# A fused FFT, squared-ReLU and mixture-of-experts kernel: w_out read back further ahead, stored rows started sooner, writes moved to earlier batches

## The chip, the core and the metric

The kernel runs on one core of one Trainium2 chip. A core has five engines, each with its own instruction stream: TensorE (PE: matrix products; PEld is its weight load), VectorE (DVE), ScalarE (ACT), GpSimd (POOL) and SyncE (SP). SP does no arithmetic here; it issues nearly all the DMAs, in program order. The metric is the device time of one execution in microseconds (us), lower is better.

## What is computed

The reference runs three stages one after the other on 8 batches of 3072 rows by 256 columns:

```python
X = np.fft.rfft(x, axis=1)                       # x: 8 x 3072 x 256
Yr, Yi = Xr @ w_r - Xi @ w_i + b_r, Xr @ w_i + Xi @ w_r + b_i
# soft threshold: sign(Y) * max(|Y| - 0.01, 0)
x = np.fft.irfft(Yr + 1j * Yi, n=3072, axis=1)   # 24576 rows
h = np.maximum(x @ w_in, 0.0)                    # w_in: 256 x 2048
x = (s * (h * h) + b) @ w_out                    # w_out: 2048 x 256
logits = x @ w_gate                              # 8 experts, capacity 768 each
# row i goes to expert argmax(logits[i]) while that has room, in order of i:
# out[i] = gate_w[i] * (max(x[i] @ w1[e], 0) @ w2[e]); rows beyond the capacity stay zero
```

Most rows end as zeros, so the kernel needs the exact middle stage for few rows. For all other rows it computes only a bounded estimate of the logits in low precision, and it clears the output by writing zeros.

## The kernel before

The main loop runs over 8 batches (b = 0 to 7), each of 64 **units**. A time in the program is written here as batch.unit: 6.42 is unit 42 of batch 6. One unit is one call of `s_unit`: four matrix products into a two-bank tile `ph` (line 786), ReLU of it on ACT into `r` (line 791), and the square on DVE into `qb` (line 792). The pool `hp` has two such tiles, and the inverse transform's tile `pi2` comes from the same two. Every eighth unit the logits are added up (`lg`, lines 806 and 809), copied by ACT to `ls`, and turned (`plt`, line 830).

Between the units stands other work, put there by a table of times. `put(at, f, rank)` enters a step `f` for a unit, and at each unit the loop first emits `s_unit`, then flushes stores left over from earlier steps (`later`), then runs the steps entered for that unit in order of rank and time. Each engine runs its own part of that sequence strictly in order. The planner's function `best` chooses, within two or three units, the one with the least booked PE work (`load[n]`) for the inverse transform (`i2_do`) and for the logits.

The steps beside the units are these.

- `groups(b + 2)`: twelve groups per batch of the transforms of a later batch. A group loads a tile `zp` from memory (line 280), makes products `pf`, `pmx`, `pi`, and stores a tile `v` (line 412). Those of batch 7 end near 6.40, after which batches 6 and 7 have only units and the work below.
- `i2_load` (line 422) loads the input `u` of the inverse transform (three buffers), and `i2_do` does it: 64 small PE instructions (line 438), a cast `ah` on ACT (line 441), two transposes on DVE (line 453), and four DMA stores of `ad` (line 458). In batch 6 the first two loads of batch 7 stand together at unit 55 (`INV_LOAD_AT`).
- Zero writes: 96 DMAs of 256 KB clear the output (line 2061), at the units in `ZERO_AT`: none in batches 0 and 1, ten in each of batches 2 to 5, 31 in batch 6 and 25 in batch 7.
- `save_in` (line 1680): four DMAs of 1 MB write the first layer's weights to memory for a rarely used path, at 6.44, 6.48, 6.52 and 6.56.
- At 6.42 (`P2_AT`) `second` frees the transforms' memory. `load_p2` then reads `w_out` back from memory in eight parts `cf` of 256 KB through three buffers. Each part goes through one cast on ACT (line 1223) and one subtraction on DVE (line 1224) into `wo`, as a high and a low half. Loads 0 and 1 are entered at 6.43 and 6.44, part k is used at 6.42 + 1 + 1.4 (k + 2), and `use(k)` issues load k + 2. When all eight are there, `g0` makes a tile of ones and `g` sums the columns of `wo` with 32 products in a row (`pbc`, line 1237); the sum `yb` is needed by the stored rows.
- Stored rows: `s_items` has 36 steps, four of start-up and 32 that do work, spread evenly between `S_FROM` (7 units before batch 7) and `S_TO` (7.62). Step k loads a tile `sq` (line 1462, three buffers shared with `cf`) for step k + 4, splits that of step k + 2 (ACT line 1469, DVE line 1470, `ssh` and `ssl`), and makes 12 products `ya` (line 1483).
- After the last unit a tail follows: routing, the experts' products, and the final scatter.

The scheduler sets a wait on SP between a DMA and the one eight DMAs before it, since it hands out eight semaphores in turn. So SP has at most eight DMAs of its queue under way, and a wait of one DMA holds all that stand behind it.

Of the kernel before, what the change touches and what calls it, by code (L numbers as in the profile page):

```python
# [10 lines left out]
F32 = mybir.dt.float32  # L11
F32R = mybir.dt.float32r
# [3 lines left out]
ALU = mybir.AluOpType  # L16
# [3 lines left out]
C = 256  # L20
# [6 lines left out]
NF = FF // 128  # L27
# [9 lines left out]
XT = NA * N2  # L37
# [84 lines left out]


FFT_CONV_AT = (0, 2, 5, 7, 10, 12, 13, 18, 20, 23, 25)
S_FROM, S_TO = -7, 62
P2_AT = 42
LIST_AT = 56
SAVE_AT = (44, 48, 52, 56)
TAIL_WARM = 3
XP = 3  # L130
INV_LOAD_AT = 55
# [5 lines left out]
LAST_STEPS = (("g_a", 0), ("g_b", 2), ("g_b2", 3), ("g_soft", 3.1), ("g_c", 5))  # L137
FIRST_STEPS = (("g_a", 0.3), ("g_b", 1.3), ("g_b2", 2), ("g_soft", 2.6), ("g_c", 5))
WORK = {"g_a": 0.87, "g_b": 1.72, "g_b2": 0.86, "g_soft": 0.0, "g_c": 0.86}
ZERO_AT = ((), (), *[tuple(range(4, 64, 6))] * 4, tuple(range(2, 64, 2)), tuple(range(8, 58, 2)))  # L140
LOGIT_LAG = 3
FIRST_LAG = 13
FIN_LAG = 2
# [13 lines left out]
class Kern:  # L157
# [1050 lines left out]
    def load_p2(self, p2):  # L1208

        nc = self.nc  # L1210
        self.wo = p2.tile([128, 2, NF, C], F32R, tag="wo", name="wo")
        st = {}

        def load(k):
            st[k] = self.p2c.tile([128, 512], F32, tag="sq", name="cf", bufs=3)
            nc.sync.dma_start(out=st[k], in_=self.wd[k])

        def use(k):
            if k + 2 < 8:
                load(k + 2)  # L1220
            s = slice(2 * k, 2 * k + 2)
            w = st.pop(k).rearrange("p (k c) -> p k c", k=2)
            nc.scalar.copy(out=self.wo[:, 0, s], in_=w)
            nc.vector.tensor_tensor(out=self.wo[:, 1, s], in0=w, in1=self.wo[:, 0, s].bitcast(F32), op=ALU.subtract)
        it = [lambda: load(0), lambda: load(1)] + [lambda k=k: use(k) for k in range(8)]

        def g0():
            t = self.p2c.tile([128, C], F32, tag="ys", name="ones3", bufs=2)
            nc.vector.memset(t, 1.0)
            st["ones"] = self.p2c.tile([128, 4, 128], F32R, tag="ssh", name="ones4", bufs=2)[:, 0]  # L1230
            nc.scalar.copy(out=st["ones"], in_=t[:, :128])

        def g():
            ps = self.psum("pbc")
            for f in range(NF):
                for w in range(2):
                    nc.tensor.matmul(ps[:, :C], st["ones"], self.wo[:, w, f], start=(f + w == 0), stop=(f == NF - 1 and w == 1))
            self.yb = p2.tile([128, C], F32, tag="yb", name="yb")
            nc.vector.tensor_scalar(out=self.yb, in0=ps[:, :C], scalar1=self.wb, scalar2=None, op0=ALU.mult)
        return it + [g0, g]  # L1240

    def full_pick(self, p2):

# [214 lines left out]

    def s_load(self, k):
        m, f = divmod(4 * k, NF)  # L1460
        t = self.p2c.tile([128, 4, 128], F32, tag="sq", name="sq", bufs=3)
        self.nc.sync.dma_start(out=t, in_=self.sd[f:f + 4].rearrange("f p n -> p f n")[:, :, 128 * m:128 * (m + 1)])
        self.sq[k] = t

# [371 lines left out]
    def run(self):  # L1836
        tc, nc, B = self.tc, self.nc, self.B
# [5 lines left out]
        with ExitStack() as es, tc.manual_schedule():  # L1843
# [79 lines left out]

            nzi, nzn = 0, sum(map(len, ZERO_AT))
            nz = B * S * C // (128 * 512)
# [30 lines left out]
            def put(at, f, rank=1):  # L1956
                e = plan.setdefault(int(at), [])
                e.append((rank, at, len(e), f))
# [14 lines left out]
            load = [0.7] * (64 * B + 80)  # L1973
# [26 lines left out]
            def plan_batch(b):  # L2000
                u = 64 * b
# [15 lines left out]
                        put(n, lambda k=k: self.x_ahead(12 + k), 0)  # L2017
                    put(18, lambda: self.x_ahead(15 + XP), 0)
                if b == B - 2:
                    for n in range(64 + S_FROM + 4, 64 + S_TO):  # L2020
                        load[u + n] += 0.7
                if b == B - 2:
                    for k, n in enumerate(SAVE_AT):
                        put(u + n, lambda k=k: self.save_in(k), 6)
                if b == 0:
# [8 lines left out]
                for i in range(8):  # L2034
                    at = u + 8 * i + 7 + LOGIT_LAG if b + i else FIRST_LAG
                    if b > 1:
                        at = best(u + 8 * i + 9, u + 8 * i + 11, 1.0)
                    if at < 64 * B:
                        put(at, lambda i=i: logits(b, i), 3)
                    if at + FIN_LAG < 64 * B:  # L2040
                        put(at + FIN_LAG, lambda i=i: final(b, i), 2)
                        load[at + FIN_LAG] += 0.4
                    if i < 7 or b + 1 < B:
                        n = best(u + 8 * i + (4 if i < 7 else 3), u + 8 * i + (6 if i < 7 else 5), 1.2, True)
                        put(n, lambda i=i: self.i2_do(*divmod(8 * b + i + 1, 8)), 5)
                    if i < 6:
                        put(u + 8 * i, lambda i=i: self.i2_load(b, i + 2), 0)
                if b == 0:
                    for k in range(8):
                        if k >= CONV_EARLY:  # L2050
# [2 lines left out]
                elif b + 2 < B:  # L2053
                    for k in range(8):
                        put(best(u + 6 * k, u + 6 * k + 4, 1.1, True), self.f1_items(b + 2)[k], 4)
                if b + 1 < B:
                    put(u + INV_LOAD_AT, lambda: (self.i2_load(b + 1, 0), self.i2_load(b + 1, 1)), 2)
                for z in range(len(ZERO_AT[b])):
                    def f(n=sum(map(len, ZERO_AT[:b])) + z):
                        for zi in range(math.ceil(nz * n / nzn), math.ceil(nz * (n + 1) / nzn)):  # L2060
# [3 lines left out]
                if b == 1:  # L2064
                    for m, j in enumerate(XB_AT):
                        w = u + 8 * j
# [13 lines left out]
            def second(at):  # L2080
                e2.close()
                p2 = es.enter_context(tc.tile_pool(name="p2", bufs=1, side="right", reuse_waits="tile"))
                self.p2c = e4.enter_context(tc.tile_pool(name="p2c", bufs=1, side="right", reuse_waits="tile"))
                self.yf = [p2.tile([128, C], F32, tag=f"yf{j}", name=f"yf{j}") for j in range(NJ)]
                u = 64 * (B - 1)
                for n, f in enumerate(self.load_p2(p2)):
                    put(at + 1 + 1.4 * n, f)
                put(at + 3, lambda: self.full_pick(p2))
                for n, f in enumerate(self.full_items(p2)):
                    put(u + 34 + 4 * n, f)  # L2090
                for k in range(4):
                    put(u + 12 + 4 * k, lambda k=k: self.exp_items(self.wx[0], self.fe)[k]())
                for j in range(NJ):
                    put(u + 44 + j, lambda j=j: self.full_gate(j))
                    put(u + S_TO, lambda j=j: self.full_rows(j))
                si = self.s_items()
                for n, f in enumerate(si):
                    put(u + S_FROM + n * (S_TO - S_FROM) / len(si), f)
                put(u + LIST_AT, self.first_block)
                return p2  # L2100
            plan_batch(0)
            for b in range(B):
                if b:
                    plan_batch(b)
                for k in range(64):
                    i, u = divmod(k, 8)
                    if (b, k) == (B - 2, P2_AT):
                        p2 = second(64 * b + k)
# [38 lines left out]
```

## Time and profile before

| | us |
|---|---|
| median of 3 runs | 1466.31 (1463.36 to 1467.7) |
| the profiled execution's own time | 1464.19 |
| its span, first to last instruction | 1462.4 |
| PE busy in the span | 1371.0 (94%) |
| DVE busy | 923.9 (63%) |
| ACT busy | 841.1 (58%) |
| batches 3, 4, 5 and 6, each | 134.0, 134.1, 136.0, 135.2 |
| batch 7's units | 117.0 |

The batches' lengths are the times between the ReLUs that begin them. PE is the busy engine, so the profile is read for the stretches in which PE is not busy, for what ended each wait, and for stretches in which the granted TensorE clock is below 1. A window row gives, for a stretch, its length, then the busy time of PE, PEld, DVE, ACT and POOL with the number of instructions, the granted clock, the mean share in which the 16 DMA engines were busy, and GB/s.

### The profile page before, as it was taken

What the parts mean: (1) busy time and instruction counts of PE and PEld (TensorE: products, weight loads), DVE (VectorE), ACT (ScalarE), POOL (GpSimd) and SP (SyncE); (2) the same over time, 40 slices, a digit from 0 to 9 for tenths busy, and PEclk for the clock granted to TensorE, in tenths of its full rate; (3) what the DMA queues carried; (4) which work ended last, traced back from release to release, by engine and by line L of the source; (5) the groups of instructions that cost most, each with busy time, mean ns of one, the idle gap of its engine ahead of it and who ended that gap; (6) DMA issues with size and microseconds to landing.
All of it is one profiled execution on the core that took longest, in us unless ns stands there. A gap on an engine that the chain in (4) does not pass through costs nothing.

```text
span 1462.4 us, 32413 instructions
## 1 busy us (share of the span) xinstructions
PE 1371.0 (94%) x12865; PEld 1133.7 (78%) x12865; DVE 923.9 (63%) x2151; ACT 841.1 (58%) x1202; POOL 99.9 (7%) x116
## 2 busy tenths in 40 slices
PE   8998799999999989999999999999999799999995
PEld 6876577787788767887888788878888588978884
DVE  1877467666555887677667667766777666664600
ACT  1436545556555656666676666666666677753321
POOL 0000000000000012002000100200020002122020
PEclk9997999999999999999999999999999999999998
DMA  8758476646454447548655865665555788840080
GB/s 236 257 173 237 106 181 171 155 131 170 140 170 121 113 110 184 157 126 187 169 153 146 190 170 131 159 175 153 139 151 162 234 221 237 224 118 16 12 313 13
DMA packets 275842, 234.51 MB, mean 160 GB/s; under 512 B 121661, under 2 KB 229951, under 8 KB 275168
## 3 DMA queue, kind: packets, MB, share of 16 engines
q1 hardware_dynamic: 269984, 226.34, 57.2%
q0 software_dynamic: 3824, 2.82, 0.8%
q10 hardware_dynamic: 1872, 3.18, 0.6%
q8 instruction: 103, 1.69, 0.5%
q14 instruction: 59, 0.48, 0.1%
HBM read 114.17 MB, written 118.29 MB: 159 GB/s over the span
## 4 chain that ended last, share of the span: by engine, by line
PE 70%; DVE 13%; ACT 6%; DMA 5%; issue 3%; SPq 2%; POOL 0%; ACTq 0%; DVEq 0%; POOLq 0%
PE ph L786 20%; PE pmx L368 14%; PE pz L246 5%; PE pi L406 4%; PE pf L291 3%; ACT r L791 3%; PE pi L438 3%; PE phx L1003 3%; PE ya L1483 3%; PE lg L806 2%; DVE qb L792 2%; PE ph L1534 2%; PE po L1544 2%; DMA zp<-zd 2%; PE ya L1018 2%
## 5 line engine op out<-in xcount | busy, mean ns | idle before, releaser
L791 ACT ACTIVATE r<-ph 128x768 bf16<-128x768 f32 (+1 forms) x512 | 399.5, 786 | 208.5 <-PE ph L786 177.8
L786 PE MATMUL ph<-ah,win 128*128 128x384 f32 (+1 forms) x2048 | 480.3, 360 | 20.5 <-ACT r L791 18.8
L792 DVE TENSOR_TENSOR qb<-r 128x768 bf16<-128x768 bf16 (+1 forms) x512 | 272.7, 534 | 245.3 <-ACT r L791 241.3
L786 PEld LDWEIGHTS ph<-ah,win 128*128 128x128 f32 x2048 | 340.6, 191 | 103.9 <-ACT r L791 42.1
L368 PE MATMUL pmx<-wm,l 128*128 128x256 f32 x1196 | 297.9, 387 | 9.4 <-DVE l L299 2.8
L368 PEld LDWEIGHTS pmx<-wm,l 128*128 128x128 f32 x1196 | 223.0, 192 | 41.0 <-ACT r L791 4.3
L940 POOL DMA_INDIRECT list<-c,x x64 | 61.3, 958 | 875.2 <-DVE c L936 858.2
L406 PE MATMUL pi<-t,e 128*128 128x256 f32 x384 | 99.3, 381 | 2.6 <-DVE t L363 1.6
L291 PE MATMUL pf<-d,zp 128*128 128x128 f32 x672 | 88.7, 275 | 1.6 <-DMA zp<-zd 1.5
L291 PEld LDWEIGHTS pf<-d,zp 128*128 128x128 f32 x672 | 85.7, 191 | 2.3 <-DMA zp<-zd 2.1
L246 PE MATMUL pz<-x,f 48*64 48x512 f32 x512 | 74.7, 653 | 10.9 <-DVE at L453 6.6
L438 PEld LDWEIGHTS pi<-f1t,u 48*64 48x64 f32 x4096 | 68.4, 136 | 18.6 <-issue 8.9
L408 ACT COPY v<-pi 128x512 f32<-128x512 f32 x96 | 56.3, 587 | 41.0 <-PE pi L406 37.7
L261 ACT COPY z<-pz 128x1024 f32<-128x1024 f32 x52 | 52.8, 1015 | 46.1 <-PE pz L246 45.9
L453 DVE STREAM_TRANSPOSE at<-pi 128x384 f32<-128x384 f32 x128 | 66.9, 561 | 19.1 <-ACT ah L441 18.0
L406 PEld LDWEIGHTS pi<-t,e 128*128 128x128 f32 x384 | 70.2, 189 | 10.8 <-DVE t L363 3.7
L438 PE MATMUL pi<-f1t,u 48*64 48x48 f32 x4096 | 76.3, 224 | 2.1 <-DMA u<-vd 1.5
L441 ACT CAST ah<-pi 128x768 fp32r<-128x768 f32 x64 | 51.3, 801 | 39.2 <-PE pi L438 39.2
L822 ACT COPY ls<-lg 128x384 f32<-128x384 f32 (+1 forms) x64 | 53.8, 841 | 32.7 <-PE lg L809 29.4
L363 DVE TENSOR_TENSOR t<-t,cl 128x512 f32<-128x512 f32 x96 | 66.6, 693 | 3.3
L1047 DVE TENSOR_TENSOR xq<-xq 128x512 f32<-128x512 f32 x48 | 33.0, 690 | 39.4 <-ACT xq L1046 39.3
L294 ACT COPY l<-pf 128x512 f32<-128x512 f32 x84 | 49.2, 586 | 10.6 <-PE pf L291 4.6
(422 smaller groups left out, 1764.4 us busy)
## 6 DMA issues: line engine op xcount, KB each, us to landing
zp<-zd SPq DMA_DIRECT2D x96, 256.0 KB
u<-vd SPq DMA_DIRECT2D x128, 192.0 KB
ad<-at SPq DMA_DIRECT2D x256, 96.0 KB
out<-zero SPq DMA_DIRECT2D x96, 256.0 KB
x<-x SPq DMA_DIRECT2D x120, 192.0 KB
vd<-v SPq DMA_DIRECT2D x84, 256.0 KB
zd<-z SPq DMA_DIRECT2D x104, 192.0 KB
sd<-xq SPq DMA_DIRECT2D x32, 256.0 KB
```

The source lines that it names most:

```text
L246: nc.tensor.matmul(ps[r][64 * k:64 * k + 64, :], self.f1[h], rhs.rearrange("p a c -> p (a c)"), start=True, stop=True, skip_group_check=True)
L291: nc.tensor.matmul(pv[:, h, :, gi * 64:gi * 64 + 64], zp[:, gi, h * 128:(h + 1) * 128], self.d[:, 2 * p + gi, :].rearrange("p (t m) -> p t ...
L363: nc.vector.tensor_tensor(out=t, in0=t, in1=cl, op=ALU.subtract)
L368: self.nc.tensor.matmul(o, part(h), w[:, h], start=start and h == 0, stop=stop and h == 1, skip_group_check=True)
L406: nc.tensor.matmul(ps[:, gi * C:(gi + 1) * C], self.e[:, 2 * p + gi], t[:, gi * C:(gi + 1) * C], start=True, stop=True)
L408: nc.scalar.copy(out=v, in_=ps)
L438: nc.tensor.matmul(o[64 * k:64 * k + 64, :, n], u[p, n, 128 * k + h:128 * k + 128:2], self.f1t[p], start=True, stop=True, skip_group_check ...
L453: nc.vector.transpose(out=at[:, :, :, h], in_=pv[:, M1 * h:M1 * (h + 1)])
L786: nc.tensor.matmul(ps[:, j, :n], self.win[:, k, f], ah[:, k, t0:], start=(k == 0), stop=(k == 1))
L791: nc.scalar.activation(out=r, in_=ps[:, :, :n], func=AF.Relu)
L792: nc.vector.tensor_tensor(out=q, in0=r, in1=r, op=ALU.mult)
L940: self.nc.gpsimd.indirect_dma_start(out=self.lists[n], out_offset=bass.IndirectOffsetOnAxis(ap=x[:, n:n + 1], axis=0), in_=c[:, n:n + 1], ...
```

## The change

Five things change, all of them in the table of times and in `load_p2`.

1. The eight parts of `w_out` get four buffers. Loads 0, 1 and 2 are entered at 6.43, 6.43 and 6.44, part k is used at 6.45 + k, one per unit, and `use(k)` issues load k + 3. The ones are made at 6.44. The four products of part k stand at 6.46 + k instead of all 32 at the end.
2. The stored rows start at 6.47 (`S_FROM` -17 instead of -7) with the same end, so a step comes every 2.19 units instead of every 1.92. Their loads have four buffers too.
3. The planner books 1.45 in each unit that has a step of the stored rows, where it booked 0.7 in every unit of their span.
4. The two first inverse loads of batch 7 stand at 6.48 and 6.56, in turn with the others, and no longer together at 6.55.
5. The four 1 MB writes go from batch 6 to batch 3 (units 10, 26, 42, 58). The zero writes become twenty in each of batches 2 to 5, 16 in batch 6 (up to unit 32) and none in batch 7. Their sum stays 96.

```diff
-S_FROM, S_TO = -7, 62
+S_FROM, S_TO = -17, 62
-SAVE_AT = (44, 48, 52, 56)
+NS_ITEMS = 4 + XT // 128 * NF // 4
+SAVE_AT = (10, 26, 42, 58)
-ZERO_AT = ((), (), *[tuple(range(4, 64, 6))] * 4, tuple(range(2, 64, 2)), tuple(range(8, 58, 2)))
+ZERO_AT = ((), (), *[tuple(range(4, 64, 3))] * 4, tuple(range(2, 34, 2)), ())
...
-            st[k] = self.p2c.tile([128, 512], F32, tag="sq", name="cf", bufs=3)
+            st[k] = self.p2c.tile([128, 512], F32, tag="sq", name="cf", bufs=4)
...
-            if k + 2 < 8:
-                load(k + 2)
+            if k + 3 < 8:
+                load(k + 3)
...
-        def g():
-            ps = self.psum("pbc")
-            for f in range(NF):
+        def add(k):
+            if k == 0:
+                st["ps"] = self.psum("pbc")
+            for f in (2 * k, 2 * k + 1):
                 for w in range(2):
-                    nc.tensor.matmul(ps[:, :C], st["ones"], self.wo[:, w, f], start=(f + w == 0), stop=(f == NF - 1 and w == 1))
+                    nc.tensor.matmul(st["ps"][:, :C], st["ones"], self.wo[:, w, f], start=(f + w == 0),
+                                     stop=(f == NF - 1 and w == 1))
...
+        it = [(k, lambda k=k: load(k)) for k in range(3)] + [(2, ones)]
+        for k in range(8):
+            it += [(3 + k, lambda k=k: use(k)), (4 + k + 0.5, lambda k=k: add(k))]
+        return it
...
-                    for n in range(64 + S_FROM + 4, 64 + S_TO):
-                        load[u + n] += 0.7
-                if b == B - 2:
+                    for n in range(4, NS_ITEMS):
+                        load[int(u + 64 + S_FROM + n * (S_TO - S_FROM) / NS_ITEMS)] += 1.45
+                if b == 3:
                     for k, n in enumerate(SAVE_AT):
...
-                    if i < 6:
-                        put(u + 8 * i, lambda i=i: self.i2_load(b, i + 2), 0)
+                    if i < 6 or b == B - 2:
+                        put(u + 8 * i, lambda i=i: self.i2_load(*divmod(8 * b + i + 2, 8)), 0)
...
-                if b + 1 < B:
+                if b + 2 < B:
                     put(u + INV_LOAD_AT, lambda: (self.i2_load(b + 1, 0), self.i2_load(b + 1, 1)), 2)
...
-                for n, f in enumerate(self.load_p2(p2)):
-                    put(at + 1 + 1.4 * n, f)
+                for n, f in self.load_p2(p2):
+                    put(at + max(1, n), f)
```

PE's order is the same up to 6.46. Then the 32 products that sum the columns of `wo` (`pbc`), which stood in a row at 6.58, stand in fours. Before, from 6.57:

```order
L786 MATMUL ph<-ah,win 128x384 x4
L1237 MATMUL pbc<-wo,ones_14069 128x256 x32
L786 MATMUL ph<-ah,win 128x384 x4
L830 MATMUL plt<-ident,ls 96x128 x4
L786 MATMUL ph<-ah,win 128x384 x4
L438 MATMUL pi_14171<-f1t,u 64x48 x32
L786 MATMUL ph<-ah,win 128x384 x16
```

The same engine after, from the inverse transform at 6.44 on; `ph` x4 is one unit:

```order
L439 MATMUL pi_13807<-f1t,u 64x48 x32
L787 MATMUL ph<-ah,win 128x384 x8
L1237 MATMUL pbc<-wo,ones_13804 128x256 x4
L787 MATMUL ph<-ah,win 128x384 x4
L1237 MATMUL pbc<-wo,ones_13804 128x256 x4
L787 MATMUL ph<-ah,win 128x384 x4
L1237 MATMUL pbc<-wo,ones_13804 128x256 x4
L787 MATMUL ph<-ah,win 128x384 x4
L1237 MATMUL pbc<-wo,ones_13804 128x256 x4
```

Eight such fours stand behind 6.46 to 6.53, and the 32 in a row are gone.

On SP, the DMA queue, the stretch from the first part of `w_out` on read before (`ws` are the 1 MB writes, `out<-zero` the zero writes, `ad` the rows of an inverse transform):

```order
L1216 DMA cf<-wd_93 128x512
L1216 DMA cf<-wd_94 128x512
L1680 DMA ws_103<-win 128x2048
L2061 DMA out<-zero 256x1x256
L458 DMA ad<-at 32x12x64 x4
L1261 TENSOR_LOAD f_ex
L1261 ISA x2
L1216 DMA cf<-wd_95 128x512
L2061 DMA out<-zero 256x1x256
L1216 DMA cf<-wd_96 128x512
L1216 DMA cf<-wd_97 128x512
L1680 DMA ws_103<-win 128x2048
```

and after:

```order
L1217 DMA cf<-wd_93 128x512
L1217 DMA cf<-wd_94 128x512
L1217 DMA cf<-wd_95 128x512
L459 DMA ad<-at 32x12x64 x4
L1217 DMA cf<-wd_96 128x512
L1266 TENSOR_LOAD f_ex
L1266 ISA x2
L1217 DMA cf<-wd_97 128x512
L1217 DMA cf<-wd_98 128x512
L1467 DMA sq<-sd 128x4x128
L423 DMA u<-vd_91 48x4x256 x2
L1217 DMA cf<-wd_99 128x512
```

The third part is now ahead of `ad`, and no write of zeros or of weights stands between the parts.

On PE in batch 7 the places of the inverse transforms (`pi`) against the stored rows (`ya`) move. At 7.12 before, two units follow the inverse transform directly:

```order
L1483 MATMUL ya<-wo,ssh 128x256 x2
L1483 MATMUL ya<-wo,ssl 128x256
L438 MATMUL pi_14377<-f1t,u 64x48 x32
L786 MATMUL ph<-ah,win 128x384 x8
L1483 MATMUL ya<-wo,ssh 128x256 x2
```

After, at the transform of 7.06 and at each later one of batch 7, one unit follows and then products of stored rows:

```order
L787 MATMUL ph<-ah,win 128x384 x8
L439 MATMUL pi_14498<-f1t,u 64x48 x32
L787 MATMUL ph<-ah,win 128x384 x4
L1488 MATMUL ya<-wo,ssh 128x256 x2
L1488 MATMUL ya<-wo,ssl 128x256
```

So the two units that stood behind one another there are parted by a `ya`.

## Rows read from the trace of the kernel before

**Rows 1.** Windows (columns above): batch 3, batch 6 to 6.40, from there to 7.00, batch 7.
```profile
649.40:783.40 134.00, 132.12 (x1304) 107.58 (x1303) 93.00 (x205) 91.81 (x120) 7.70 (x8) 1.00 0.65 162
...
1053.50:1142.00 88.50, 87.09 (x816) 72.31 (x815) 66.05 (x148) 53.32 (x72) 7.42 (x8) 1.00 0.58 155
1142.00:1188.70 46.70, 36.14 (x397) 29.96 (x398) 27.47 (x56) 31.92 (x48) 0.00 (x0) 0.93 0.89 277
1188.70:1305.70 117.00, 112.59 (x1264) 103.48 (x1263) 76.57 (x162) 84.81 (x117) 16.23 (x16) 1.00 0.73 199
```
**Rows 2.** Waits of PE, 1142.0 to 1188.7: us in total, times, longest.
```profile
PE ph L786 <- ACT r L791: 9.6, 6, 3.0
...
PE pi L438 <- ACT r L791: 0.6, 1, 0.6
PE pbc L1237 <- ACT ones L1231: 0.3, 1, 0.3
```
**Rows 3.** Waits of ACT, same stretch.
```profile
ACT wo L1223 <- DMA cf<-wd: 5.9, 3, 2.6
```
**Rows 4.** Timeline, PE's long stalls: start, us, what [idle before it <- releaser].
```profile
1155.11 1.68 PE L786 MATMUL ph<-ah,win 128*128 128x384 f32 x8 [2.28 <-ACT r L791]
...
1160.94 1.65 PE L786 MATMUL ph<-ah,win 128*128 128x384 f32 x4 [2.33 <-ACT r L791]
...
1165.06 1.18 PE L438 MATMUL pi<-f1t,u 48*64 48x48 f32 x64 [0.58 <-ACT r L791]
...
1170.22 4.61 PE L786 MATMUL ph<-ah,win 128*128 128x384 f32 x16 [2.98 <-ACT r L791]
```
**Rows 5.** Timeline of SP's queue: issue time, us that the issues took.
```profile
1148.35 1.37 SPq L1216 DMA_DIRECT2D cf<-wd  x2
1149.78 0.46 SPq L1680 DMA_DIRECT2D ws<-win  x1
...
1151.35 4.48 SPq L458 DMA_DIRECT2D ad<-at  x4
```
**Rows 6.** Windows of 5 us with the clock below 1.
```profile
1160.00:1165.00 5.00, 3.54 (x12) 3.08 (x12) 2.48 (x4) 3.58 (x7) 0.00 (x0) 0.66 0.80 302
...
1170.00:1175.00 5.00, 4.78 (x24) 4.22 (x28) 3.61 (x8) 4.40 (x8) 0.00 (x0) 0.66 1.01 316
```
**Rows 7.** Timeline: first cast; a ReLU, cast and subtraction; the 32 products.
```profile
1153.73 0.62 ACT L1223 CAST wo<-cf 128x512 fp32r<-128x512 f32 x1 [1.88 <-issue]
...
1164.21 0.80 ACT L791 ACTIVATE r<-ph 128x768 bf16<-128x768 f32 x1
...
1164.91 0.61 ACT L1223 CAST wo<-cf 128x512 fp32r<-128x512 f32 x1
...
1165.55 0.69 DVE L1224 TENSOR_TENSOR wo<-cf,wo 128x512 fp32r<-128x512 f32 x1
...
1176.93 4.10 PE L1237 MATMUL pbc<-wo,ones 128*128 128x256 f32 x32 [0.28 <-ACT ones L1231]
```
**Rows 8.** Chain that ended last: two units in a row; a late stored row.
```profile
1202.51 1.40 PE ph L786 x8
...
1222.35 5.86 DMA sq<-sd
```
**Rows 9.** Waits of PE in batch 7, 1188.7 to 1305.7.
```profile
PE ph L786 <- ACT r L791: 4.4, 6, 0.9
```
**Rows 10.** Windows of eight units: transform and stored row together; apart.
```profile
1204.00:1219.40 15.40, 14.50 (x170) 13.21 (x169) 10.45 (x28) 11.20 (x17) 7.43 (x8) 1.00 0.80 207
...
1235.60:1249.70 14.10, 14.10 (x167) 13.18 (x166) 9.19 (x17) 10.87 (x15) 0.00 (x0) 1.00 0.94 264
```
**Rows 11.** Timeline: the unit after next behind a transform, 6.62.
```profile
1185.77 1.66 PE L786 MATMUL ph<-ah,win 128*128 128x384 f32 x8 [0.90 <-ACT r L791]
```
**Rows 12.** Timeline, batch 3: issue of a `zp` on SP, its products on PE.
```profile
690.48 1.30 SPq L280 DMA_DIRECT2D zp<-zd  x1
...
704.24 1.05 PE L291 MATMUL pf<-d,zp 128*128 128x128 f32 x8
```

## The prediction on record

> **What bounds the kernel now.** I read the windows by stage first, then the waits in the stage that stands out, then the timeline of that stage, then SP's queue. The reader is to see in [rows 1] that PE is busy 132.12 of 134.00 us in batch 3 (batches 4 to 6 are like it) and 87.09 of 88.50 us in batch 6 up to 6.40. There only PE's work counts. In the next 46.70 us PE is busy for only 36.14 us, at a mean clock of 0.93 and with the DMA engines 0.89 busy. Then batch 7 has 112.59 of 117.00 us. Both stretches together last 163.7 us, with 148.7 us of PE's work and 15.0 us without any. This is what the change can get at.
>
> The waits name one partner: PE waits 9.6 us in six waits for the ReLU on ACT, and 0.6 us in a seventh [rows 2]. ACT is not slow; it is held itself. It waits 5.9 us for parts of w_out [rows 3], and 1.88 us before the first cast [rows 7], whose part was issued at 1148.35 and whose cast ran only at 1153.73 [rows 5, 7]. The cast stands between two ReLUs in ACT's order, so a late part holds the ReLU, and with two tiles of `hp` the second unit after it holds PE. In SP's queue the 1 MB write is issued 0.06 us behind the first two parts, and the four stores behind it take 4.48 us to issue [rows 5], since each waits for a DMA eight places before.
>
> **What the change removes.** Four stalls of PE belong to late parts [rows 4]: 2.28 + 2.33 + 0.58 + 2.98 = 8.2 us. Two 5 us windows have a clock of 0.66 [rows 6]: in each the clock is at 1.2 instead of 2.4 GHz for 3.4 us, right after the stalls, and that costs 2 x 5 x 0.34 = 3.4 us of work at full clock; I take 3.3, since PE was idle for a little of it. The wait of the 32 products for the ones is 0.28 us [rows 7]; ones are now made at 6.44, so it goes.
>
> The new order of inverse transforms removes a second kind of wait. Where two units follow a transform directly, the second waits 0.90 us, because ACT does the cast of the transform before the ReLU of the first [rows 11]. In batch 7 the waits are 4.4 us in six [rows 9]; in the timeline four of them are such 0.90 us waits, behind the transforms of 7.04, 7.12, 7.44 and 7.52. Where a stored row stands between the two units the ReLU has time: eight units then take 14.10 us without any idle, against 15.40 us with 0.90 idle [rows 10]. The changed order has that form at every transform from 6.54 on, so 4 x 0.90 = 3.6 us go in batch 7. Ahead of it the six waits of 9.6 us [rows 2] less the three long ones of 7.6 [rows 4] leave 2.0: 0.90 and 0.20 behind the transform of 6.60, which go, and 0.90 behind that of 6.44. A transform in the same unit as `plt` (7.36) also has one unit and then a stored row behind it. The one at 6.44 still has two units behind it and keeps its wait.
>
> A stored row that came late because its load did is on the chain with 5.86 us [rows 8], but most of that lies beside PE's work; PE waits 0.6 us there. I count 0.6. With the zero writes gone from batch 7 and a fourth buffer it goes.
>
> Sum removed: 8.2 + 3.3 + 0.3 + 3.6 + 1.1 + 0.6 = 17.1 us.
>
> **What it adds.** Most edits have one answer. The number of casts, subtractions, products, loads and writes is the same; four stored rows (12 products each) move from batch 7 into the end of batch 6, which moves time and adds none. The load of 7.0 at 6.48 waits for nothing that is late: its buffer is free since the transform two before, and its `vd` has been stored by 6.43.
>
> New is a wait of PE for each part. Products of part k stand one unit behind its cast. From the start of a ReLU the cast starts 0.70 us later, the subtraction 0.64 us after that, and it takes 0.69 us [rows 7]: with 0.1 us for the hand-over 2.1 us from the end of a unit to its products. In that time PE has one more unit, 0.70 us [rows 8]. A pair of units then lasts about 2.1 + 0.70 + a group of four products, 4.10/8 = 0.51 us [rows 7], so 3.3 us, against 2 x (0.70 + 0.51) = 2.4 us of work. Over four pairs that is 3.6 us idle; the logits and the turning that fall among them take some 1.5 us of PE's time and fill part, but ACT gets their copy too. I take 3.0 us. The ends are 0, if PE runs far enough behind, and 6.0, if each of eight groups waits 0.75 us.
>
> Also new is that parts are needed one unit apart, not 1.4. Between 6.43 and 6.56, some 20 us, SP issues eight parts and five stored tiles of 256 KB, one `vd`, four loads of `u` at 192 KB and eight stores at 96 KB: 5.2 MB, or 260 GB/s. The stage ran at 302 and 316 GB/s where it was saturated [rows 6], so this fits, with little to spare. Each part has a lead of three units, about 5 us. The first had 5.4 us with 1 MB and zeros around it [rows 5, 7] and was 1.88 us late. I take 0.5 us; the ends are 0 and 3.
>
> The moved writes go where they are covered. A `zp` of batch 3 is issued at 690.48; by the program it is used six units later, which is at 704.24 [rows 12]. That is a lead of 13.8 us against the 5.4 us of the slow part above. The other loads are issued as early. A batch of 2 to 5 gets 2.6 MB more and batch 3 4.2 MB besides: 162 GB/s over 134 us [rows 1] are 21.7 MB, and they become 28.5 MB or 213 GB/s, below what the DMA engines gave above. Batch 6 had a zero write every two units and PE busy 98% [rows 1]. Cost 0, ends -1 and 3.
>
> **The sum.** 17.1 - 3.0 - 0.5 = 13.6 us. The profiled execution took 1464.19 us, which is 1.8 us over its span, and so becomes 1450.6 us. It lies 2.1 us under the median of the three runs, 1466.31; against that the changed kernel takes 1452.7, say 1453 us.
>
> **Rivals.**
>
> *The wait moves to the products.* If each of the eight groups waits its upper value (6.0 us) and the clock falls once more behind it (3.3 us in place of none), the gain is 17.1 - 6.0 - 0.5 - 3.3 = 7.3 us, and the time 1459 us. For it speaks that the chain ReLU, cast, subtraction, products is longer than a unit. Against it, the clock fell only behind stalls of 2 to 3 us [rows 4, 6], and the waits expected here are a third of those. The Trainium skill, page "TensorE: Matmul & The Clock Gate", section "HAM oscillation — how this bites in real kernels", speaks against dealing products out: it advises to do a contraction's steps together before waiting for the next data, so that the engine stays at full clock. By that rule this rival is the likely one; the rows show that the 32 products together did not save the clock before, since the fall came with the stalls ahead of them.
>
> *Parts and stored tiles still come late.* If half of the 8.2 us stays and one of two slow-clock stretches (1.7 us), the gain is 13.6 - 4.1 - 1.7 = 7.8 us, 1458.5 us. For it: 260 GB/s wanted in bursts. Against it: 277 GB/s over 46.7 us [rows 1] were 12.9 MB, and the four 1 MB writes and the 11 zero writes that the table has there, 7 MB of them, are gone.
>
> *Both of these, so that nothing measurable is left.* 17.1 - 9.3 - 3 - 4.1 = 0.7 us, to about 1465 us.
>
> *Slower: the 1 MB writes hold the queue in batch 3.* SP was held 4.48 us behind one such write [rows 5]. If PE loses that at each of the four, it costs 17.9 us; less the gain of 13.6 the kernel takes 1470.6 us. It decides from the point at which a `zp` comes over 13.8 us after its issue, 8.4 us later than the slow part did. The Trainium skill, page "DMA: Bandwidth & Descriptors", section "Queues, rings and completion order", says that each DMA engine consumes descriptors in ring order, so a load does stand behind a write issued before it; by that rule alone, with no lead, this rival would be right. No row of batch 3 shows such a write.
>
> **How the numbers follow.** The forecast (gain of 10 to 17 us) 0.60, the products' wait 0.13, late parts 0.14, both together 0.07, slower 0.06. A measurement of this kernel tells 0.3%, or 4.4 us, from no change. Faster by more: 0.60 + 0.13 + 0.14 = 0.87; same 0.07; slower 0.06. The forecast's own range is 1449 to 1457. All of 17.1 us, and a gain of 1 in the moved writes, would give 1448; the low end is 1447, to allow for the spread of runs. The high end takes in the two middle rivals with some late parts more, 1462. Outside lie the last two rivals.
>
> **What the profile after would show.** From 1142 to 7.00 no wait of a cast for `cf`, and clock 1.00. Eight groups of four `pbc`, with waits for the subtraction on DVE of 0.3 to 0.8 us: more than 6 us in all means the first rival. In batch 7 no 0.90 us waits behind transforms, and eight units in about 14 us. Batch 3 still at 134 us: at 138 or more the slower rival is at work. If the gain were in batches 2 to 5, or the tail after 7.63 changed by more than 2 us, the reasoning would be wrong.

## The result

The changed kernel takes 1450.39 us (median of 6 runs, 1446.2 to 1455.21), the kernel before, run beside it, 1466.07 us (6 runs, 1459.92 to 1467.7). The ratio is 0.9897, with an interval of 0.9875 to 0.9918. The forecast was 1453 us.

Both profiles split by the same marks, the starts of the ReLUs that begin the units (us). "Stage" is the stretch from 6.42, where `w_out` begins to be read back, to 7.63; it holds the same work in both kernels, and is the measure of all comparisons below.

| | to batch 1 | 1 | 2 | 3 | 4 | 5 | 6 to 6.42 | stage | tail | span |
|---|---|---|---|---|---|---|---|---|---|---|
| before | 301.3 | 201.3 | 146.8 | 134.1 | 134.0 | 136.0 | 92.9 | 159.2 | 156.7 | 1462.4 |
| after | 299.4 | 201.5 | 143.5 | 134.0 | 134.0 | 136.1 | 92.9 | 147.7 | 157.9 | 1447.1 |

So 15.3 us = 11.5 (stage) + 3.3 (batch 2) + 1.9 (start) - 1.2 (tail), and small change. In the start the order is the same in both kernels, and it varied from 298.8 to 309.9 us in the kernels below, so the 1.9 us lie within that scatter and are not counted as the change's.

Windows of the changed kernel, with the columns of [rows 1]: batch 3, batch 6 to 6.40, from there to 7.00, batch 7, the tail.

```profile
644.40:778.50 134.10, 132.21 (x1305) 107.69 (x1305) 93.12 (x205) 91.86 (x121) 7.71 (x8) 1.00 0.77 213
1048.60:1137.00 88.40, 87.03 (x816) 72.27 (x814) 65.96 (x148) 53.27 (x72) 7.43 (x8) 1.00 0.55 147
1137.00:1181.90 44.90, 40.73 (x444) 34.75 (x445) 30.67 (x61) 34.63 (x51) 0.00 (x0) 0.96 0.62 156
1181.90:1289.20 107.30, 106.55 (x1215) 97.23 (x1215) 73.52 (x156) 83.11 (x112) 17.23 (x17) 1.00 0.58 143
1289.20:1447.10 157.90, 130.21 (x1043) 113.14 (x1041) 51.54 (x201) 42.79 (x82) 31.26 (x31) 0.95 0.26 87
```

The stretch of [rows 1] that PE spent 15.0 us of its 163.7 without work is now 44.9 + 107.3 = 152.2 us with 4.9 us idle. Batch 3 carries 213 GB/s in place of 162 and is as long as before.

Waits of PE after (us in total, times, longest), from 6.40 to 7.00 and then in batch 7, to be held against [rows 2, 9]; ACT has no wait for `cf` left against the 5.9 us of [rows 3]:

```profile
PE pbc L1237 <- DVE wo L1225: 1.6, 5, 0.3
PE ph L787 <- ACT r L792: 1.5, 1, 1.5
PE pbc L1237 <- ACT wo L1224: 1.0, 4, 0.3
PE pi L407 <- DVE t L364: 0.8, 1, 0.8
...
PE ph L787 <- ACT r L792: 0.4, 2, 0.2
PE pi L439 <- ACT r L792: 0.2, 1, 0.2
```

The clock did not stay at 2.4 GHz throughout. Two windows of 5 us behind the first products are at 0.84 and 0.82, that is (0.16 + 0.18) x 5 x 2 = 3.4 us at 1.2 GHz; the timeline shows what PE and ACT did just ahead of them:

```profile
1146.00:1151.00 5.00, 3.36 (x14) 2.45 (x14) 4.22 (x13) 3.63 (x7) 0.00 (x0) 0.84 0.68 169
1151.00:1156.00 5.00, 4.42 (x27) 3.72 (x31) 3.18 (x6) 3.46 (x6) 0.00 (x0) 0.82 0.81 252
```
```profile
1145.06 0.30 ACT L1230 CAST ones<-ones 128x128 fp32r<-128x128 f32 x1 [0.90 <-DVE ones L1228]
...
1146.82 0.96 PE L787 MATMUL ph<-ah,win 128*128 128x384 f32 x4 [1.50 <-ACT r L792]
...
1148.79 0.62 PE L1237 MATMUL pbc<-wo,ones 128*128 128x256 f32 x3 [0.34 <-DVE wo L1225]
```

ACT waits 0.90 us for DVE's ones, and only then casts the transform of 6.44; PE's wait behind that transform is 1.50 us where it was 0.90.

### The profile page after: what moved, and what is told of

It reads as the page before. It is cut to its first block, busy times and chain, and to the rows that moved or that the text cites. A ratio compares the mean times of both kernels' runs of the same rounds, so it can differ in the third digit from the quotient of the medians.

```text
span 1447.1 us, 32414 instructions
## 1 busy us (share of the span) xinstructions
PE 1365.4 (94%) x12865; PEld 1127.6 (78%) x12865; DVE 923.3 (64%) x2151; ACT 841.9 (58%) x1202; POOL 100.6 (7%) x116
## 4 chain that ended last, share of the span: by engine, by line
PE 73%; DVE 13%; ACT 6%; issue 3%; DMA 3%; SPq 0%; POOL 0%; ACTq 0%; DVEq 0%; POOLq 0%
PE ph L787 21%; PE pmx L369 15%; PE pz L247 5%; PE pi L407 5%; PE pi L439 3%; PE pf L292 3%; PE ya L1488 3%; PE phx L1004 3%; ACT r L792 3%; PE lg L807 2%; PE ph L1539 2%; DVE qb L793 2%; PE po L1549 2%; PE ya L1019 2%; PE plt L831 2%
## 5 line engine op out<-in xcount | busy, mean ns | idle before, releaser
L442 ACT CAST ah<-pi 128x768 fp32r<-128x768 f32 x64 | 51.3, 801 | 38.8 <-PE pi L439 38.8
L445 ACT ACTIVATE asq<-ah 128x768 bf16<-128x768 f32 x64 | 53.6, 837 | 1.4 <-PE lg L810 1.4
```

## The experiments

The stage of every kernel, from one profile each, and its ratio to the kernel before with a 95% interval. e1 to e10 ran on one chip, e11 to e13 on a second. The stage is the finer of the two: the start alone varies by 11 us (298.8 to 309.9). The ratios follow the stages roughly: kernels with a stage of 153 us or more lie at 0.9917 to 0.9966, those with 151 us or less at 0.9873 to 0.9917. But only e2's interval is clear of the changed kernel's, and e1's touches it; all other differences to the changed kernel rest on the profiles.

| kernel | 6.42 to 7.00 | batch 7 | stage | ratio |
|---|---|---|---|---|
| before | 42.2 | 117.0 | 159.2 | |
| after | 40.5 | 107.3 | 147.7 | 0.9897 [0.9875, 0.9918] |
| e1: before, only the writes moved | 36.5 | 116.6 | 153.1 | 0.9942 [0.9918, 0.9966] |
| e2: after, all writes back | 48.6 | 107.3 | 155.9 | 0.9966 [0.9942, 0.9989] |
| e3: after, the 32 products in a row | 42.8 | 107.3 | 150.1 | 0.9892 [0.9856, 0.9927] |
| e4: after, stored rows' start and booking undone | 36.4 | 116.9 | 153.3 | 0.9932 [0.9906, 0.9957] |
| e6: after, only the 1 MB writes back | 41.0 | 107.3 | 148.3 | 0.9917 [0.9889, 0.9945] |
| e7: after, ones first, products a unit later | 41.4 | 107.3 | 148.6 | 0.9886 [0.9850, 0.9923] |
| e8: after, only the start undone | 35.7 | 113.5 | 149.2 | 0.9897 [0.9843, 0.9951] |
| e10: after, parts two ahead | 46.1 | 107.3 | 153.3 | 0.9917 [0.9895, 0.9939] |
| e11: after, only the zero writes back | 42.5 | 108.5 | 151.0 | 0.9897 [0.9858, 0.9936] |
| e12: after, ones first | 39.7 | 107.3 | 147.0 | 0.9909 [0.9876, 0.9941] |
| e13: e12, parts 1.25 units apart | 38.8 | 107.3 | 146.0 | 0.9873 [0.9843, 0.9902] |

In the kernels with the early start four more steps of the stored rows stand ahead of 7.00 (5.8 us of PE's work: it is busy for 106.55 us in batch 7 after, for 112.36 us in e8), so the first two columns compare only among kernels with the same start.

### e1: the writes alone

```diff
-SAVE_AT = (44, 48, 52, 56)
+SAVE_AT = (10, 26, 42, 58)
-ZERO_AT = ((), (), *[tuple(range(4, 64, 6))] * 4, tuple(range(2, 64, 2)), tuple(range(8, 58, 2)))
+ZERO_AT = ((), (), *[tuple(range(4, 64, 3))] * 4, tuple(range(2, 34, 2)), ())
```

(and `save_in` entered in batch 3.)

> The kernel before with the moved writes alone (zero writes and the four 1 MB writes where the changed kernel has them; nothing else changed). Theory 'queue': the parts of w_out came late because those writes shared the queue, so the waits of the cast for cf (7.8 us of ACT before) nearly go, PE's stalls of 8.2 us shrink under 2 us, the clock may still fall once; 6 to 10 us faster than before, 1456 to 1460 us. Theory 'lead': the parts came late because only two were under way; then at most 2 us faster, 1464 us, with the waits for cf at 5 us or more. If the 3 us that batch 2 lost in the changed kernel (3.3 us by its trace) are due to the moved zero writes, batch 2 has them here too.

Measured: 159.2 to 153.1 us. The stage up to 7.00, and ACT's wait for parts in it:

```profile
1149.30:1185.80 36.50, 29.57 (x363) 23.62 (x362) 23.81 (x49) 27.50 (x42) 0.00 (x0) 1.00 0.64 151
...
ACT wo L1223 <- DMA cf<-wd: 2.9, 1, 2.9
```

Moving the writes gives 6.1 us by itself: the clock is 1.00, and of 5.9 us in three waits for parts one of 2.9 is left. Batch 7 keeps its waits behind transforms (3.8 us in five).

### e2: all writes back

The same edit, the other way, in the changed kernel.

> The changed kernel with all writes back where they stood before. 'Queue': waits of ACT for cf or sq come back, 6 to 10 us slower than the changed kernel, 1456 to 1460 us. 'Lead': the fourth buffer and the third part ahead cover them, within 2 us of the changed kernel, 1450 to 1452 us.

```profile
1152.20:1200.70 48.50, 40.94 (x410) 34.92 (x409) 27.79 (x54) 31.39 (x45) 0.00 (x0) 0.86 0.91 283
...
ACT wo L1224 <- DMA cf<-wd: 4.1, 3, 1.9
```

Against the changed kernel 8.2 us are lost: parts come late again, and the clock falls to 0.86 on average. Without the moved writes all the rest of the change is worth 159.2 - 155.9 = 3.3 us.

### e6 and e11: which writes

e6 puts back only the 1 MB writes, e11 only the zero writes (the lines of `SAVE_AT` with its batch, and of `ZERO_AT`, reversed).

> The changed kernel with only the four 1 MB writes back at 6.44 to 6.56; the zero writes stay where the change puts them. All writes back made the stage from 6.42 to 7.63 8.2 us longer (155.9 against 147.7). If the 1 MB writes hold the parts, most of that returns: stage 153 to 156 us, a granted clock of 0.85 to 0.93 up to 7.00, and casts that wait for parts 3 us or more. If it is the zero writes, the stage is 148 to 149 us. For batch 2 (146.8 us before, 150.0 with all writes back, 143.5 with the writes moved): the zero writes of batch 2 stand as in the changed kernel, so 143.5 if they set it.

> The changed kernel with only the zero writes where they were before (ten in each of batches 2 to 5, 31 in batch 6, 25 in batch 7); the four 1 MB writes stay in batch 3. With all writes back the stage from 6.42 to 7.63 was 155.9 us, with only the 1 MB writes back 148.3, in the changed kernel 147.7. If it is the zero writes that hold the parts, the stage is 154 to 156 us, casts wait for parts 3 us or more and the granted clock up to 7.00 is 0.90 or less. If it is the sum of both kinds (the 1 MB writes alone drew 264 GB/s without harm, both 279 GB/s with it), zeros alone fit as well: 148 to 149 us. Batch 2 was 146.8 and 150.0 us in the two kernels that had ten zero writes in it and 142.9 to 143.5 us in the eight that have twenty: it is 146 to 150 us here if their places set it, 143 if not.

Up to 7.00, e6 and then e11: windows, ACT's first wait for a part, and SP's queue (start, us) at the first parts.

```profile
1144.20:1185.20 41.00, 36.53 (x410) 31.46 (x409) 27.64 (x54) 30.93 (x45) 0.00 (x0) 0.96 0.88 264
...
ACT wo L1224 <- DMA cf<-wd: 0.7, 2, 0.4
...
1144.81 1.39 SPq L1217 DMA_DIRECT2D cf<-wd  x3
1146.24 0.43 SPq L1685 DMA_DIRECT2D ws<-win  x1
```
```profile
1147.80:1190.30 42.50, 37.02 (x411) 32.00 (x410) 27.55 (x54) 30.95 (x46) 0.00 (x0) 0.92 0.80 224
...
1148.46 1.22 SPq L2066 DMA_DIRECT2D out<-zero  x2
1149.78 2.08 SPq L1217 DMA_DIRECT2D cf<-wd  x3
...
1155.69 0.62 ACT L1224 CAST wo<-cf 128x512 fp32r<-128x512 f32 x1 [1.83 <-DMA cf<-wd]
```

The 1 MB writes alone cost 0.6 us, though they make the DMA engines busier (264 GB/s, 0.88) than the zero writes do (224 GB/s, 0.80). The zero writes alone cost 3.3 us: 2.0 up to 7.00, and 1.3 in batch 7, where stored rows come late. Up to 7.00 the queue tells the two apart: in e6 three parts are issued ahead of the first write, in e11 two zero writes stand ahead of them, and the first cast is 1.83 us late. In the kernel before two zero writes stand there too, which the reading of [rows 5] left out. The queue before, then e11 in batch 7:

```profile
1147.05 1.20 SPq L2061 DMA_DIRECT2D out<-zero  x2
```
```profile
1235.19 0.62 ACT L1474 CAST ssh<-sq 128x512 fp32r<-128x512 f32 x1 [1.95 <-DMA sq<-sd]
...
1240.56 1.18 PE L439 MATMUL pi<-f1t,u 48*64 48x48 f32 x64 [1.01 <-ACT r L792]
```

Both kinds together cost 8.2 us, about twice the sum of 0.6 and 3.3, and e11's 151.0 us lies between its two expectations. So neither theory holds alone: writes ahead of the first parts go with their lateness, and both kinds together cost more than each by itself. The total times do not show e11's loss (0.9897, as the changed kernel). The Trainium skill states (page "DMA: Bandwidth & Descriptors", section "Queues, rings and completion order") that each DMA engine consumes descriptors in ring order. e11 fits that but does not show it, since SP's issue of the two writes takes 1.22 us by itself, and that too puts off the parts.

### e3: the products in a row

```diff
-            it += [(3 + k, lambda k=k: use(k)), (4 + k + 0.5, lambda k=k: add(k))]
+            it += [(3 + k, lambda k=k: use(k)), (12.5, lambda k=k: add(k))]
```

> The changed kernel with the 32 products in a row again, behind the last part at 6.54. If dealing them out costs by the chain ReLU, cast, subtraction, products: PE's waits of 2.6 us for wo go, and the clock stays at 1.00 between 1143 and 1156; 2 to 4 us faster than the changed kernel, 1446 to 1448 us. If dealing out helps by filling PE while ACT casts: units there become bound by ACT, and the time is the same or up to 3 us more, 1450 to 1453 us.

```profile
PE ph L787 <- ACT r L792: 5.3, 5, 1.9
...
ACT wo L1224 <- DMA cf<-wd: 3.5, 3, 1.7
```

The first of the two expectations fell: dealt out, the stage is 2.4 us shorter in these two profiles, though the ratios (0.9892 and 0.9897) do not tell the kernels apart. The 2.6 us of waits in front of the products are gone here, but with nothing between them the units come faster than the parts, ACT waits 3.5 us for these, and PE 5.3 us for ACT. The clock up to 7.00 is 0.92 against 0.96. The advice of the Trainium skill (page "TensorE: Matmul & The Clock Gate", section "HAM oscillation — how this bites in real kernels") to do a contraction's steps together before waiting for the next data finds no support in this pair.

### e10: two parts ahead

```diff
-name="cf", bufs=4)
+name="cf", bufs=3)
-            if k + 3 < 8:
-                load(k + 3)
+            if k + 2 < 8:
+                load(k + 2)
```

(two first loads in place of three, and three buffers for the stored rows too.)

> The changed kernel with the parts read back two ahead through three buffers, as before, in place of three through four; stored rows have three buffers too. All else is as in the changed kernel, the products dealt out too. If the third part ahead is needed once the parts come one unit apart, ACT waits for parts 2 us or more and the stage from 6.42 to 7.63 is 150 us or more. If moving the writes was enough, no cast waits for a part and the stage is 147.5 to 148.5 us, the time as that of the changed kernel, about 1450 us.

```profile
PE pbc L1237 <- ACT wo L1224: 3.8, 3, 2.3
...
ACT wo L1224 <- DMA cf<-wd: 3.0, 3, 1.9
```

The third part ahead is worth 5.6 us of stage (153.3 against 147.7) where parts come one unit apart.

### e4 and e8: the stored rows

e8 undoes the start (`S_FROM` -17 to -7); e4 also undoes the booking (0.7 in every unit of the span in place of 1.45 at the steps).

> The changed kernel with the stored rows starting at the old time and booked as before (parts 2 and 3 of the change undone). My reckoning: the 0.90 us waits behind inverse transforms come back in batch 7 (four) and at its edge (one), 4 to 6 us slower than the changed kernel, 1454 to 1456 us; batch 7's idle on PE back to about 4 us. Rival: those waits were due to the writes' traffic and stay away; within 1 us of the changed kernel.

> The changed kernel with the stored rows begun 7 units ahead of batch 7 as before, but the planner's booking (1.45 in each unit that has a step) kept. With start and booking both undone the stage from 6.42 to 7.63 was 153.3 us, with both 147.7. If the booking is what parts the two units behind a transform, batch 7's waits of 0.90 us behind transforms go, and the stage is about 149.5 us (3.6 us less than 153.3). If the earlier start does it (other distances of the steps), the four waits stay and the stage is 153 us. Batch 7's own length is some 5.7 us longer than in the changed kernel under both, as four stored rows stand in it again.

PE's waits in batch 7, e4 and then e8, with the late stored row behind the longer of e8's two; then e8's window up to 7.00 and PE's waits in it:

```profile
PE ph L786 <- ACT r L791: 3.8, 5, 0.9
```
```profile
PE ph L787 <- ACT r L792: 1.1, 2, 0.9
...
1225.26 0.62 ACT L1474 CAST ssh<-sq 128x512 fp32r<-128x512 f32 x1 [4.03 <-DMA sq<-sd]
...
1226.64 0.97 PE L787 MATMUL ph<-ah,win 128*128 128x384 f32 x4 [0.89 <-ACT r L792]
```
```profile
1153.90:1189.60 35.70, 30.04 (x363) 24.32 (x362) 24.14 (x49) 28.32 (x42) 0.00 (x0) 1.00 0.64 155
...
PE ph L787 <- ACT r L792: 3.2, 5, 1.5
```

The booking does it: the four 0.90 us waits behind transforms go with the planner's rule, and the 0.89 us left in e8 is another kind, behind a late stored row. The stage is 4.1 us shorter (153.3 to 149.2), 3.4 of it in batch 7; the other 0.7 goes with a fall of the clock that e4 has ahead of 7.00 and e8 has not. The earlier start adds 1.5 us. e4 also has the deeper lead and the dealt-out products, and is no better than e1 (153.3 and 153.1): its parts are no longer late, but 1.5 us of waits in front of the products and a fall of the clock (0.95) stand in the place of e1's 2.9 us. One wait took the place of another.

### e7, e12 and e13: the waits in front of the products

```diff
-        it = [(k, lambda k=k: load(k)) for k in range(3)] + [(2, ones)]
+        it = [(0, ones)] + [(k, lambda k=k: load(k)) for k in range(3)]
```

That is e12. e7 also enters the products at 5 + k + 0.5; e13 uses part k at 3 + 1.25 k and adds it at 5 + 1.25 k.

> The changed kernel with two edits: each group of four products stands one unit further behind its part's cast, and the ones are made ahead of the first load, not behind the third. In the changed kernel PE waits 2.6 us for the casts and subtractions in front of the products and 1.5 us behind the transform of 6.44, where the ones' cast stands ahead of the unit's; its clock then falls once for 3.4 us (1.7 us of work). Theory A (these waits cost what they show): the stage from 6.42 to 7.63 goes from 147.7 to 143 to 145 us, the waits in front of the products are under 0.5 us, the one behind 6.44 is 0.9 us, the clock there is 1.00, and the time is about 1446 us. Theory B (the waits only pass on the parts' pace: with the products in a row PE ran faster and the parts came later): the parts are late by as much, ACT waits for them 2 to 3 us, and the stage stays at 147 to 150 us. Rows of batch 7 are as in the changed kernel under both.

> The changed kernel with the ones made ahead of the first load. In the changed kernel ACT's cast of the ones waits 0.9 us for DVE and stands ahead of the cast of the transform of 6.44, and PE waits 1.50 us behind that transform; the clock fell 2.6 us after that for 3.4 us. If that wait brings the fall, the wait is 0.9 us, the clock up to 7.00 is 1.00 and the stage from 6.42 to 7.63 is 145 to 146 us (147.7 in the changed kernel). If the fall comes from the products' waits (2.6 us in nine), it stays and the stage is 147 us.

> The changed kernel with the ones made first, the parts used 1.25 units apart in place of one, and each group of four products two units behind its cast. With two units and parts one unit apart the parts came 3.3 us late and the stage from 6.42 to 7.63 was 148.6 us. If the parts' rate was the limit there (256 KB of part a unit, beside stored tiles, inputs and stores), a quarter more time lets all be there: no cast waits for a part, the products wait under 0.5 us, the clock is 1.00 and the stage is 143.5 to 145 us; the time is then 1445 to 1449 us beside a median of 1466 to 1473 for the kernel before. If the waits only move (parts still late, or the stored rows that begin right behind the last part wait for it), it is 147 us or more.

Up to 7.00: e7's wait for parts and PE's waits in front of the products, e12's window, e13's window and wait for parts.

```profile
ACT wo L1224 <- DMA cf<-wd: 3.3, 3, 2.4
...
PE pbc L1237 <- DVE wo L1225: 1.8, 4, 0.7
...
PE pbc L1237 <- ACT wo L1224: 1.2, 1, 1.2
```
```profile
1148.50:1188.20 39.70, 35.20 (x411) 30.04 (x410) 27.66 (x54) 30.94 (x46) 0.00 (x0) 1.00 0.67 168
```
```profile
1149.10:1187.90 38.80, 35.68 (x410) 31.69 (x410) 27.52 (x54) 30.87 (x46) 0.00 (x0) 0.96 0.67 172
...
ACT wo L1224 <- DMA cf<-wd: 1.9, 2, 1.3
```

e7 answers for theory B: with the products a unit later the parts are late by 3.3 us, 3.0 us of waits in front of the products remain, and the stage is 148.6. In e12 the clock is 1.00; the waits in front of the products (2.9 us) did not make it fall. But its stage, 147.0, is an us longer than I had expected with that. e13 is the shortest stage, 146.0, between its two expectations, with parts still 1.9 us late.

### The changed kernel again, on another chip

> The changed kernel itself once more, as the measure of how much of a difference between two profiles is chance. All experiments are compared with one profile of it, in which the stage from 6.42 to 7.63 took 147.7 us with one fall of the clock (3.4 us at half). If that stage repeats, it is 147.2 to 148.2 us and the differences of 3 us and more between the experiments are their edits'. If the fall of the clock and the parts' arrival vary from one execution to the next, it is anywhere from 146 to 149 us, and the differences of 0.6 to 1.7 us (the 1 MB writes, the ones, the wider parts, the products one unit later) are not to be told from chance. Batch 2 should be 142.9 to 143.5 us again, and the ratio to the kernel before 0.987 to 0.992.

This run fell on another chip of the same kind, on which the kernel before takes 1530.18 us (11 runs) and the changed one 1519.88 (6 runs): 0.9927, 0.9899 to 0.9955, 10.3 us less, a ratio just above the expected range. The stretch from 6.42 to 7.00 took 39.6 us against 40.5. So differences under 1 us (e6, e7, e12) can't be told from chance, and e13's 1.7 us barely; that e13 beats the changed kernel is not shown by its times either, whose intervals overlap. Batch 7 was 12.4 us longer there; of that, and of batch 2, the last section tells.

## Why the prediction was right, and where it was not

**Where the time is.** Right for the stage: a net gain of 13.6 us was forecast, 11.5 were measured. Batches 3 to 5 and the tail (1.2 us) stayed within what was said. But the total came so close to the forecast because batch 2 gave 3.3 us more, which no step foresaw: that is luck, and the prediction had itself named a gain in batches 2 to 5 as a sign against its reasoning.

**Late parts (8.2), the ones (0.3), transforms in batch 7 (3.6), 6.60 (1.1), the late stored row (0.6).** All these waits are gone. The forecast left 15.0 - 13.8 + 3.5 = 4.7 us without work; 4.9 are left. The 3.6 us come from the booking, as e8 shows: by it a stored row stands between the two units.

**The clock (3.3).** This is the term that was mis-sized. I let both falls go; one came back. PE's busy time over [rows 1]'s stretch fell from 148.73 to 147.28 us, so 1.45 were gained, not 3.3. [Rows 4, 6] had falls behind stalls of 2 to 3 us alone; this one came 2.6 us behind one of 1.50. That stall I had in hand and didn't count: the transform of 6.44 "keeps its wait", and the ones' cast was put ahead of it, which made 0.90 into 1.50 us. The other kernels bear out the link only in part. Nine profiles have the 1.50 us wait, and in seven of them the clock falls within 3 us of its end (in e2 and e11 with other long waits beside it); of the five with 0.90 or 0.96 us there, none has a fall at that place. But e3 and e8 have the 1.50 us and no fall behind it, and in e8 the clock is 1.00 up to 7.00. So the longer wait goes with the fall and does not settle it; what does stays open.

**The products' wait (3.0).** 2.6 us in nine waits, 0.2 to 0.3 each. The size was right, the first rival's (6.0) was not. Late parts, put at 0.5, cost nothing. But these waits are not a loss that could simply be had back: in e3, which takes them away, and in e7, which was to, the parts are late by 3.5 and 3.3 us instead.

**Moved writes (0).** Right for batches 2 to 5 as a cost. In e8's profile PE waits 2.02 us in batch 3 for a `zp`, and the batch takes 136.6 us. In the nine other kernels with these writes in batch 3 it takes 134.0 to 134.4, the last chip left out. That looks like the slower rival but is not shown to be: this `zp` was issued 0.66 us ahead of the first 1 MB write, and came 12.2 us after its issue, while POOL issued indirect DMAs. Beside these the DMA engines moved 45 GB/s in e8, and 38 GB/s at the same place before, where no 1 MB write stands. The rows of e8, and the last one of before:

```profile
675.88 0.61 SPq L281 DMA_DIRECT2D zp<-zd  x1
676.54 1.75 SPq L1685 DMA_DIRECT2D ws<-win  x1
...
688.04 2.07 PE L292 MATMUL pf<-d,zp 128*128 128x128 f32 x8 [2.02 <-DMA zp<-zd]
...
680.20:684.20 4.00, 4.00 (x38) 3.42 (x40) 1.76 (x4) 2.21 (x3) 2.87 (x4) 1.00 0.73 45
```
```profile
675.20:678.20 3.00, 3.00 (x19) 2.81 (x18) 1.56 (x4) 1.40 (x2) 2.08 (x4) 1.00 0.69 38
```

The tail may bear a cost: it takes 156.7 and 156.5 us in before and e2, which have all writes where they were, and 157.7 to 161.6 in the others on those chips; no run tells why. The reading of [rows 5] that the 1 MB write holds the parts was only half right: e6 shows that behind three parts it costs 0.6 us.

**What made the gain.** By undoing in turn: the writes 6.1 us (159.2 to 153.1), lead, dealing out and inverse loads together nothing more as long as the rows start late (153.3), the booking 4.1 (149.2), the start 1.5 (147.7). From the other end, with the rows early, the lead is worth 5.6 us and dealing out 2.4, so the early start seems to need them. The inverse loads were not undone alone.

## What to carry to other kernels

Read in the DMA queue what stands ahead of a load that is on the path, not only how busy the DMA engines are: up to 7.00, four 1 MB writes that began behind three loads cost 0.5 us at 264 GB/s, and 256 KB writes, two of them ahead of these loads, 2.0 us at 224. Before counting a wait as a loss, ask what would come next if it went: here, without the waits in front of the products, the parts came late instead (e3). And where a planner places work, tell it which unit is full; here a booking of the right unit gave more (4.1 us) than starting that work earlier (1.5).

## What the runs showed of the hardware

**ACT stands still beside POOL's indirect DMAs.** Batch 2 took 146.8, 150.0 and 146.6 us in the three kernels with ten zero writes in it (before, e2, e11), and 142.9 to 143.5 in the ten with twenty, other than on the last chip. In each of the three ACT idles at 2.30 ahead of the copy `l`, which by the program waits only for PE's `pf`, finished long before. The copy in before, and POOL's last indirect DMA of a run of eight; then the same two in e11; then the copy after, where nothing idles:

```profile
581.66 0.59 ACT L294 COPY l<-pf 128x512 f32<-128x512 f32 x1 [2.63 <-PE pz L246]
...
580.25 1.03 POOL L940 DMA_INDIRECT list<-c,x  x1 [0.30 <-issue]
```
```profile
583.13 0.59 ACT L295 COPY l<-pf 128x512 f32<-128x512 f32 x1 [2.97 <-PE pz L247]
...
581.38 1.02 POOL L941 DMA_INDIRECT list<-c,x  x1 [0.30 <-issue]
```
```profile
577.55 0.58 ACT L295 COPY l<-pf 128x512 f32<-128x512 f32 x1
```

ACT goes on 0.4 and 0.7 us after POOL's run has ended. The DMA engines move little beside that run: 19 GB/s from 576.6 to 580.6 us before, but also only 43 GB/s from 575.2 to 579.2 us after, where ACT does not idle. On the other chip such stalls come in every batch from 2 on; in batch 3, which takes 139.8 us there:

```profile
697.51 0.81 ACT L823 COPY ls<-lg 128x384 f32<-128x384 f32 x1 [6.38 <-remote]
...
696.34 0.92 POOL L941 DMA_INDIRECT list<-c,x  x1 [0.30 <-issue]
```

There PE halts too, inside two transforms of batch 7, for nothing that the profile names, while POOL issues indirect DMAs or up to 1.7 us later:

```profile
PE pi L439 <- issue: 6.5, 10, 1.1
```

The rest of the 12.4 us there is PE's busy time, 112.50 against 106.55 us, at a clock of 0.96. On the first chips the stall of batch 2 goes with its zero writes: it comes in all three kernels with ten, in none of the ten with twenty, and e11, which moves the zero writes alone, takes 3.1 us more there than the changed kernel (146.6 against 143.5). Why is open. In e2 ACT goes on only 2.3 us after POOL's run, so its end is not the whole of it.
